# A circular convolution fed tile by tile into an MLP: the inverse transform's chain begins some chunks earlier, and its roundings are queued behind named gelus

## The chip, the core and the metric

The kernel runs on one core of a Trainium2 chip. The metric is device time in microseconds, the median of the runs. Engines are named as the profile names them: PE (TensorE, with its weight loads as PEld), DVE (VectorE), ACT (ScalarE), POOL (GpSimd), SP (SyncE, which here only issues DMAs). Each engine takes its instructions in the order of its own queue. ACT and POOL issue DMAs too, from the same queue as their arithmetic.

## The reference

```python
# 8 batches, 3008 tokens, 256 channels, 2048 hidden
X = np.fft.rfft(x, axis=1)
F = (filt_r + 1j * filt_i)[None, :, :]
y = np.fft.irfft(X * F, n=x.shape[1], axis=1).astype(np.float32)
x = y.reshape(B * S, D)
h = x @ w_in
g = h * (1.0 / (1.0 + np.exp(-1.702 * h)))
out = (g @ w_out).astype(np.float32)
```

All of it is float32. The kernel multiplies float32r parts: a value is rounded to a high part, and the rest is kept as a low part, so that one product becomes three passes (high x high, high x low, low x high).

## The kernel before

The tokens are cut into 48 **tiles** of up to 512 tokens, `tiles[j] = (b, t)`, with batch b = 0 to 7 and t = 0 to 5; a tile with t = 5 and even b is 384 wide. The tiles' MLP is what PE does most of the time. Per tile it runs over NFC = 16 **chunks** of 128 hidden units. For a chunk fc:

- `first(fc)`: six matmuls h<-y,wi (L782) into a PSUM bank of a ring of three (two of its own and one shared); then ACT's gelu twice, gh (L785, rounded) and in place (L786), then DVE's gl = h - gh (L787), after which the bank is free for the next chunk but two.
- `second(fc)`: four matmuls o<-gh,wo and two o<-gl,wo (L806). The two gl matmuls are held back into the next chunk.
- after chunk 15 ACT copies one PSUM bank of o out (L813) and DVE the other (L814), and SP stores them (L824). There are two o banks, so the next tile's `second(0)` needs both copies.

The **turns** loop (L876) numbers all chunks n = 0, 1, 2, ...; from tile 2 on, n = 16 j + fc. In turn n it traces `first` of chunk n + 2 (`ahead`), then `second` of chunk n, then a share of the next batch's forward transform, then steps of the next tile's signal.

**fft(b)** computes the filtered spectrum of batch b while batch b - 1 is in the MLP. For b > 1 its first half is `packed` (s matmuls L537, eviction by ACT L539 and DVE L540/L541, DMA to a_d issued by ACT L468); its second half reads a_d (zy loads issued by POOL L574), has 16 steps of `forward`/`backward` (matmuls L588, merges L596/L597, product L605, L610 to L612, splitting L616/L617) and writes b_d (DMA issued by ACT L633). Its filter comes in f_buf, a pair of buffers that SP loads two steps ahead (`load_f`, issued at L208). It is spread over the turns by a list of costs.

**turned_signal(b, t, y)** (L721), for the 35 tiles with b > 0 and t > 0, makes the tile's input y from b_d. It is a generator; each `yield` ends a step:

1. load: `br` by two DMAs from SP (L731, issued at L208);
2. rounding: for m = 0, 1 ACT copies br to bh (L737), and POOL subtracts bl = br - bh (L738);
3. and 4. passes: for m = 0, 1 three matmuls i<-bh, bl, bh (L305 to L307) and DVE's transpose into zt (L746);
5. write: zt to DRAM (z_d<-zt, SP);
6. reads: four DMAs y<-z_d (SP), into the tile y, which has two buffers;
7. and 8. for m = 0, 1 `split_off` (L714): ACT rounds y's high part (L718), POOL subtracts its low part (L719).

For t = 0, or b = 0, `signal` (L652) does the work with other steps; the change leaves their turns as they are.

Steps of tile i + 1 are run during tile i (the tile ahead of it), in the turns fc of the list `at` (L909): (0, 2, 3, 4, 5, 7, 11, 12) for a turned signal, one step at each.

What sets the order on an engine: the program is traced in the order of the source, and a scheduler then places the instructions into the engines' queues by a simulated timeline, earlier-traced ones first whenever several are ready in it. It may so place an instruction far ahead of where it was traced if its inputs and buffers are ready in the simulation. `keep_in_program_order` pins an instruction against the others that are pinned on its engine (the first matmul of the passes, the transform's matmuls, early loads). br and zt share seven `raw` buffers with the transform, and bh and bl seven `half` buffers.

Of the kernel before, what the change touches and what calls it, by code (L numbers as in the profile page):

```python
# [13 lines left out]
AF = mybir.ActivationFunctionType  # L14
# [153 lines left out]
def tile_kernel(  # L168
# [545 lines left out]
    def split_off(y, m, q, to=None):  # L714

        to = y[:, :, m, q] if to is None else to
        src = y[:, 1, m, q].bitcast(F32)
        nc.scalar.copy(to[:, 0], src)  # L718
        nc.gpsimd.tensor_tensor(to[:, 1], src, to[:, 0].bitcast(F32), ALU.subtract)  # L719

    def turned_signal(b, t, y):  # L721

        if not t2_two:
            t2_two.append(const.tile([P, 2, P], F32R, name="t2_two"))
            nc.scalar.copy(t2_two[0][:, 0], t2_sb)
            nc.vector.tensor_tensor(t2_two[0][:, 1], t2_sb, t2_two[0][:, 0].bitcast(F32), ALU.subtract)
        t2h, t2l = (t2_two[0][:, k] for k in range(2))
        br = raw(f"br_{b}_{t}")
        for j in range(2):
            n = NH * j + 4 * t  # L730
            load_in(br[64 * j : 64 * j + 64], b_of[b][n : n + 4].rearrange("n k d -> k n d"))  # L731
        yield
        es = []
        for m in range(2):
            eh, el = half(f"bh_{b}_{t}_{m}"), half(f"bl_{b}_{t}_{m}")
            src = br[:, 2 * m : 2 * m + 2]
            nc.scalar.copy(eh, src)  # L737
            nc.gpsimd.tensor_tensor(el, src, eh.bitcast(F32), ALU.subtract)  # L738
            es.append((eh, el))
        yield  # L740
        zt = sb.tile([P, 8, 4, 32], F32, tag="raw", name=f"zt_{b}_{t}", bufs=7)
        for m in range(2):
            ps = ring("f", [P, 2, D], f"i1_{b}_{t}_{m}")
            mm3(ps, t2h, t2l, *es[m])
            to = zt[:, :, 2 * m : 2 * m + 2].rearrange("p c q i -> p q c i")
            nc.vector.transpose(to, ps.rearrange("p q (c i) -> p q c i", c=8))  # L746
            yield
        z_d = dram.tile([P, 8, P], F32, tag="z_d", name=f"z_d_{b}_{t}")
        load_in(z_d, zt.rearrange("p c q i -> p c (q i)"))
        yield  # L750
        src = z_d.rearrange("(a j) (k g) e -> g j k a e", a=4, g=4)
        for g in range(4):
            dst = y[32 * g : 32 * g + 32, 1].bitcast(F32)
            load_in(dst.rearrange("p k (a e) -> p k a e", a=4), src[g])
        yield
        for m in range(2):
            if t < 5 or b % 2:
                split_off(y, m, slice(0, 512))
            if t == 5 and b % 2:
                for k in range(2):  # L760
                    gap = slice(352 + 128 * k, 384 + 128 * k)
                    nc.gpsimd.tensor_copy(y[:, :, m, gap], carry[:, :, m, 32 * k : 32 * k + 32].bitcast(F32))
            elif t == 5:
                split_off(y, m, slice(0, 352))
                split_off(y, m, slice(384, 416), y[:, :, m, 352:384])
                split_off(y, m, slice(416, 480), carry[:, :, m])
            yield

    def mlp(b, t, y, nb, sums):

        w = P * nb
        pos, gs, held = [], {}, []

        def first(fc):
            ps = ring("h", [P, 512], f"h_{b}_{t}_{fc}")
            half, o = divmod(fc, HALF)
            c = slice(P * o, P * o + P)  # L780
            for n, (kc, wk, yk) in enumerate([(k, *q) for k in range(2) for q in ((0, 0), (0, 1), (1, 0))]):
                nc.tensor.matmul(ps[:, :w], wi_sb[half][:, wk, kc, c], y[:, yk, kc, :w], start=n == 0, stop=n == 5)  # L782
            gh = sb.tile([P, 512], F32R, tag="gh", name=f"gh_{b}_{t}_{fc}", bufs=3)
            gl = sb.tile([P, 512], F32R, tag="gl", name=f"gl_{b}_{t}_{fc}", bufs=3)
            nc.scalar.activation(gh[:, :w], ps[:, :w], AF.Gelu_apprx_sigmoid)  # L785
            nc.scalar.activation(ps[:, :w], ps[:, :w], AF.Gelu_apprx_sigmoid)  # L786
            nc.vector.tensor_tensor(gl[:, :w], ps[:, :w], gh[:, :w].bitcast(F32), ALU.subtract)  # L787
            gs[fc] = gh, gl

        def second(fc, hold):  # L790
            if fc == 0:
                pos.extend(p.tile([P, 512], F32, tag=k, name=f"o_{b}_{t}_{m}") for m, (p, k) in enumerate(sums))
                if sums[0][0] is ps_x:
                    shared[0] = None
            gp = gs.pop(fc)
            wo = wo_sb[fc // HALF][:, fc % HALF]
            order = held[:]
            order += [(m, wo[:, wk], gp[0], fc == wk == 0, False) for wk in range(2) for m in range(2)]
            if fc == NFC - 1:
                order.sort(key=lambda q: q[0])  # L800
            held[:] = [(m, wo[:, 0], gp[1], False, fc == NFC - 1) for m in range(2)]
            if not hold:
                order += held
                held.clear()
            for m, wb, g, first_one, last_one in order:
                ins = nc.tensor.matmul(  # L806
                    pos[m][:, :w], wb[:, P * m : P * m + P], g[:, :w], start=first_one, stop=last_one
                )
                if (b, t, fc) == (*tiles[-1], NFC - 1):
                    tc.keep_in_program_order(ins)  # L810
            if fc == NFC - 1:
                o = sb.tile([P, 2, 512], F32, tag="out", name=f"out_{b}_{t}")
                nc.scalar.copy(o[:, 0, :w], pos[0][:, :w])  # L813
                nc.vector.tensor_copy(o[:, 1, :w], pos[1][:, :w])  # L814
                for m in (0, 1) if (b, t) == tiles[-1] else (slice(0, 2),):
                    stores.append((out[:, m, done_w[0] : done_w[0] + w], o[:, m, :w]))
                done_w[0] += w

        return first, second
# [6 lines left out]
    def run(gen, n=None):  # L826
        while n is None or n > 0:
            if next(gen, run) is run:
                return False
            n = None if n is None else n - 1  # L830
        return True
# [1 line left out]

    carry = const.tile([P, 2, 2, 64], F32R, tag="carry", name="carry")
    b_t = []
    ys, t2_two = {}, []

    def start(b, t):
        ys[b, t] = sb.tile([P, 2, 2, 512], F32R, tag="y", name=f"y_{b}_{t}")
        return (turned_signal if b and t else signal)(b, t, ys[b, t])  # L840
# [27 lines left out]
    def width(i):  # L868
        return 4 if tiles[i][1] < 5 or tiles[i][0] % 2 else 3

    legs, passed, since = [], 0, 0
    for b in range(B - 1):
        upto = sum(NFC * width(i) for i in range(6 * b + 6)) - 4 * LEAD - (12 * width(6 * b + 5) if b else 26)
# [2 lines left out]
    for n, (i, fc) in enumerate(turns):  # L876
        b, t = tiles[i]
        if n == 0:
            run(start(*tiles[1]))
        if n == 2 * NFC:  # L880
            shared[0] = "f"
        if n == 6 * NFC:
            shared[0] = "h"
        while begun <= min(n + 1 + (n >= 6 * NFC), len(turns) - 1):
            ahead(*turns[begun])
            begun += 1
        chunks_of[i][1](fc, turns[n + 1 : n + 2] == [(i, fc + 1)])
        if fc == 1:
            store()
        if n < 26:  # L890
            run(conv, 1)
            if n % 2 and n < 12:
                load_unit(EARLY + 9 + n // 2)
        if n == 11:
            split_de()
            in_order[0] = False
        if n == 26:
            zy.append(const.tile([P, 4, 2, 2, D], F32R, tag="zy", name="zy"))
        if n >= LEAD and legs:
            passed += width(i)  # L900
            costs, steps, upto = legs[0]
            while steps and sum(costs) - sum(steps) + steps[0] <= sum(costs) * (passed - since) / (upto - since) + 0.01:
                run(nxt[0], 1)
                steps.pop(0)
            if not steps:
                legs.pop(0)
                nxt[0] = fft(B - len(legs)) if legs else None
                since = upto
        at = (0, 2, 3, 4, 5, 7, 11, 12) if t < 5 and b else (1, 3, 9) if t < 5 else (8, 11, 12) if b else (9, 12, 13)  # L909
        if n in (23, 26, 27) or i > 1 and fc in at and i + 1 < len(tiles):  # L910
            i = max(i, 1)
            if i + 1 not in sigs:
                sigs[i + 1] = start(*tiles[i + 1])
            run(sigs[i + 1], 1)
            if n == 27 or i > 1 and fc == at[-1]:
                run(sigs[i + 1])
    store()


# [26 lines left out]
```

## Time and profile before

| | us |
|---|---|
| median of 3 runs (2362.40 to 2367.47) | 2364.46 |
| the profiled execution's own time | 2361.29 |
| its span, first to last instruction | 2359.5 |
| PE busy | 2337.6 (99%) |
| DVE busy | 1612.2 (68%) |
| ACT busy | 1385.0 (59%) |
| POOL busy | 1106.1 (47%) |
| granted TensorE clock | 1.00 |

The profile is one execution. An engine's busy time counts its arithmetic; waits and DMA issues are not in it. PE's matmuls are pipelined, and the end of each is modelled, so that a matmul's shown length is longer than the step from one to the next; an idle time of PE is shown shorter than it is by that difference. A wait is put down to what came last.

### The profile page before, as it was taken

The page shows a single profiled execution, that of the slowest core. Times are in us where ns is not written, and L with a number is a line of the kernel's source. Part 1 is how long each engine was busy: PE and PEld are TensorE (multiplying, and loading weights), DVE is VectorE, ACT ScalarE, POOL GpSimd, SP SyncE. Part 2 cuts the span into 40 slices and gives each one's busy share as a digit, 9 for nine tenths or more (in the row PEclk, how much of TensorE's full clock was granted, in tenths as well). Part 3 has the DMA queues.
Part 4 walks back from the last instruction along what each step waited for, and adds up shares of the span by engine and source line. Part 5 has one row for each costly group of instructions (what it writes and reads, how often), then busy time and mean ns, then how long its engine had stood idle before and what let it go on. Part 6 is the DMA issues. An engine that isn't in the chain of part 4 may idle for free.

```text
span 2359.5 us, 32148 instructions
## 1 busy us (share of the span) xinstructions
PE 2337.6 (99%) x10680; PEld 1945.0 (82%) x10680; DVE 1612.2 (68%) x2476; ACT 1385.0 (59%) x2572; POOL 1106.1 (47%) x979
## 2 busy tenths in 40 slices
PE   9999999999999999999999999999999999999999
PEld 7878898887888878888888877978888888788887
DVE  7978867787676776768767677676876687732322
ACT  6666656566565656656666566565666566544443
POOL 3035546455554555646555455545656455510110
PEclk9999999999999999999999999999999999999999
DMA  9275545565445664465544655455654555421110
GB/s 334 81 196 109 110 108 136 117 150 128 116 134 119 137 134 110 130 136 132 118 131 132 129 118 123 116 149 113 146 135 115 134 130 119 103 59 39 55 41 18
DMA packets 183077, 285.50 MB, mean 121 GB/s; under 512 B 18176, under 2 KB 119680, under 8 KB 182912
## 3 DMA queue, kind: packets, MB, share of 16 engines
q1 hardware_dynamic: 106208, 172.96, 25.5%
q0 software_dynamic: 46592, 44.05, 11.5%
q10 hardware_dynamic: 30112, 66.44, 11.2%
q8 instruction: 85, 1.39, 0.3%
q14 instruction: 80, 0.66, 0.1%
HBM read 171.18 MB, written 112.20 MB: 120 GB/s over the span
## 4 chain that ended last, share of the span: by engine, by line
PE 80%; DVE 4%; DMA 3%; issue 2%; POOL 1%; ACT 1%; SPq 1%; ACTq 0%; DVEq 0%; POOLq 0%
PE o L806 36%; PE h L782 36%; PE i L588 2%; PE s L588 2%; DMA y<-z_d 2%; PE s L537 1%; DVE gl L787 1%; PE i L700 1%; SPq L208 1%; DMA z_d<-zt 1%; DMA br<-b_d 1%; PE i L305 1%; PE i L307 1%; PE i L306 1%; POOL c_buf L612 1%
## 5 line engine op out<-in xcount | busy, mean ns | idle before, releaser
L782 PE MATMUL h<-y,wi 128*128 128x512 f32 (+1 forms) x4608 | 1176.8, 386 | 9.8 <-DVE gl L787 9.3
L782 PEld LDWEIGHTS h<-y,wi 128*128 128x128 f32 x4608 | 857.0, 188 | 180.0 <-DVE gl L787 18.1
L787 DVE TENSOR_TENSOR gl<-h,gh 128x512 fp32r<-128x512 f32 (+1 forms) x768 | 520.1, 679 | 500.9 <-ACT h L786 429.4
L806 PE MATMUL o<-gh,wo 128*128 128x512 f32 (+1 forms) x3072 | 835.8, 385 | 2.7 <-ACT gh L785 2.7
L785 ACT ACTIVATE gh<-h 128x512 fp32r<-128x512 f32 (+1 forms) x768 | 451.9, 588 | 520.8 <-PE h L782 417.8
L806 PEld LDWEIGHTS o<-gh,wo 128*128 128x128 f32 x3072 | 573.7, 188 | 114.1 <-ACT gh L785 4.6
L806 PE MATMUL o<-gl,wo 128*128 128x512 f32 (+1 forms) x1536 | 484.0, 385 | 0.3 <-DVE gl L787 0.3
L786 ACT ACTIVATE h<-h 128x512 f32<-128x512 f32 (+1 forms) x768 | 448.7, 584 | 0.0
L617 POOL TENSOR_TENSOR zy<-c_buf,zy 48x512 fp32r<-48x512 f32 x224 | 319.9, 1428 | 74.5 <-DVE zy L616 64.3
L806 PEld LDWEIGHTS o<-gl,wo 128*128 128x128 f32 x1536 | 287.5, 188 | 56.3 <-DVE gl L787 1.1
L612 POOL TENSOR_TENSOR c_buf<-c_buf,u_buf 112x512 f32<-112x512 f32 x112 | 144.6, 1291 | 260.9 <-DVE c_buf L611 260.9
L738 POOL TENSOR_TENSOR bl<-br,bh 128x512 fp32r<-128x512 f32 x70 | 92.4, 1328 | 289.2 <-ACT bh L737 283.0
L574 POOL DMA_DIRECT2D zy<-a_d x224 | 130.2, 586 | 168.9 <-PE s L588 60.6
L597 DVE TENSOR_TENSOR c_buf<-s,c_buf 48x512 f32<-48x512 f32 x224 | 154.0, 688 | 37.7 <-ACT c_buf L596 32.1
L719 POOL TENSOR_TENSOR y<-y 128x512 fp32r<-128x512 f32 (+1 forms) x76 | 90.7, 1212 | 169.4 <-ACT y L718 169.4
L597 DVE TENSOR_TENSOR b<-i,b 48x512 f32<-48x512 f32 x224 | 153.6, 686 | 19.2 <-ACT b L596 13.9
L596 ACT COPY c_buf<-s 48x512 f32<-48x512 f32 x224 | 130.2, 581 | 55.9 <-PE s L588 27.0
L596 ACT COPY b<-i 48x512 f32<-48x512 f32 x224 | 130.1, 581 | 40.5 <-PE i L588 32.1
L539 ACT CAST a<-s 64x512 fp32r<-64x512 f32 x144 | 83.7, 581 | 83.9 <-PE s L537 51.4
L616 DVE CAST zy<-c_buf 48x512 fp32r<-48x512 f32 x224 | 97.1, 434 | 49.9 <-POOL c_buf L612 45.5
L540 DVE TENSOR_TENSOR a<-s,a 64x512 f32<-64x512 f32 x144 | 99.0, 688 | 46.4 <-ACT a L539 43.4
L526 POOL TENSOR_TENSOR e<-x,e 64x512 fp32r<-64x512 f32 x72 | 94.7, 1316 | 46.6 <-DVE e L525 25.0
(128 smaller groups left out, 1779.1 us busy)
## 6 DMA issues: line engine op xcount, KB each, us to landing
f_buf<-fs SPq DMA_DIRECT2D x224, 192.0 KB, 3.4
zy<-a_d POOLq DMA_DIRECT2D x224, 192.0 KB, 3.6
a_d<-a ACTq DMA_DIRECT2D x144, 256.0 KB, 3.0
x<-in_x_dram SPq DMA_DIRECT2D x47, 512.0 KB, 5.3
out_dram<-out SPq DMA_DIRECT2D x43, 512.0 KB, 3.6
b_d<-b ACTq DMA_DIRECT2D x112, 192.0 KB, 2.6
br<-b_d SPq DMA_DIRECT2D x84, 256.0 KB, 4.5
z_d<-zt SPq DMA_DIRECT2D x35, 512.0 KB, 2.7
```

The source lines that it names most:

```text
L540: nc.vector.tensor_tensor(lo, ps[t], a[t, 0], ALU.subtract)
L574: nc.gpsimd.dma_start(zy[0][64 * k : 64 * k + 48, i % 2].rearrange("p k s d -> p (k s) d"), src)
L596: nc.scalar.copy(dst[h], ps[o])
L597: nc.vector.tensor_tensor(dst[h], ps[h], dst[h], ALU.add)
L612: nc.gpsimd.tensor_tensor(u1, u1, u2, ALU.add)
L616: nc.vector.tensor_copy(y[h, k], u1[h])
L617: nc.gpsimd.tensor_tensor(y[o, k], u1[h], y[h, k].bitcast(F32), ALU.subtract)
L782: nc.tensor.matmul(ps[:, :w], wi_sb[half][:, wk, kc, c], y[:, yk, kc, :w], start=n == 0, stop=n == 5)
L785: nc.scalar.activation(gh[:, :w], ps[:, :w], AF.Gelu_apprx_sigmoid)
L786: nc.scalar.activation(ps[:, :w], ps[:, :w], AF.Gelu_apprx_sigmoid)
L787: nc.vector.tensor_tensor(gl[:, :w], ps[:, :w], gh[:, :w].bitcast(F32), ALU.subtract)
L806: ins = nc.tensor.matmul(pos[m][:, :w], wb[:, P * m : P * m + P], g[:, :w], start=first_one, stop=last_one)
```

## The change

A list `gelu` collects every second gelu instruction (L786) as it is traced. Two kinds of ACT copies of the turned signal, the rounding (L737) and the one of `split_off` (L718), are traced inside `tc.issue_after(gelu[-1])`: on ACT's queue they stand behind the newest gelu traced so far, wherever else the scheduler puts them. No semaphore is added, since both are on ACT. In turn n the newest traced gelu is that of chunk n + 2.

The turns of the steps are no longer read from the tile that runs, but listed ahead in `due`, by the tile j that they are for, counted from the first turn of the tile ahead, 16 (j - 1). For a turned signal they become (-6, -2, -1, 0, 1, 3, 9, 10) instead of (0, 2, 3, 4, 5, 7, 11, 12): the load 6 turns earlier, rounding, passes, write and reads 4 earlier, `split_off` 2 earlier. The first steps so lie in the last turns of the tile before the tile ahead. The other signals keep their turns.

```diff
@@ split_off
-        nc.scalar.copy(to[:, 0], src)
+        with tc.issue_after(gelu[-1]):
+            nc.scalar.copy(to[:, 0], src)
@@ turned_signal
-            nc.scalar.copy(eh, src)
+            with tc.issue_after(gelu[-1]):
+                nc.scalar.copy(eh, src)
@@ mlp, first
-            nc.scalar.activation(ps[:, :w], ps[:, :w], AF.Gelu_apprx_sigmoid)
+            gelu.append(nc.scalar.activation(ps[:, :w], ps[:, :w], AF.Gelu_apprx_sigmoid).ins)
@@ tile_kernel
-    ys, t2_two = {}, []
+    ys, t2_two, gelu = {}, [], []
...
+    due = {}
+    for j in range(2, len(tiles)):
+        b, t = tiles[j]
+        if j == 2:
+            steps = 23, 26, 27
+        else:
+            at = (-6, -2, -1, 0, 1, 3, 9, 10) if b and t else (1, 3, 9) if t else (8, 11, 12) if b > 1 else (9, 12, 13)
+            steps = [NFC * (j - 1) + k for k in at]
+        for n in steps:
+            due.setdefault(n, []).append(j)
...
-        at = (0, 2, 3, 4, 5, 7, 11, 12) if t < 5 and b else (1, 3, 9) if t < 5 else (8, 11, 12) if b else (9, 12, 13)
-        if n in (23, 26, 27) or i > 1 and fc in at and i + 1 < len(tiles):
-            i = max(i, 1)
-            if i + 1 not in sigs:
-                sigs[i + 1] = start(*tiles[i + 1])
-            run(sigs[i + 1], 1)
-            if n == 27 or i > 1 and fc == at[-1]:
-                run(sigs[i + 1])
+        for j in due.pop(n, ()):
+            if j not in sigs:
+                sigs[j] = start(*tiles[j])
+            run(sigs[j], 1)
+            if not any(j in later for later in due.values()):
+                run(sigs[j])
```

## Rows read from the trace of the kernel before

**Rows 1.** The page, busy time of each engine (share of the span) and instructions.
```profile
PE 2337.6 (99%) x10680; PEld 1945.0 (82%) x10680; DVE 1612.2 (68%) x2476; ACT 1385.0 (59%) x2572; POOL 1106.1 (47%) x979
```

**Rows 2.** Busy time by stretch: from:to, length, busy (instructions) per engine, clock, DMA.
```profile
340.00:2060.00 1720.00, 1705.77 (x7661) 1417.84 (x7660) 1245.02 (x1894) 1039.65 (x1915) 940.01 (x831) 1.00 0.53 127
...
2160.00:2220.00 60.00, 60.00 (x267) 1.00 0.12 36
```

**Rows 3.** Waits of PE, 340 to 2060 us: total us, times, longest us.
```profile
PE h L782 <- DVE gl L787: 8.9, 9, 2.6
PE i L588 <- POOL zy L617: 2.9, 9, 0.5
```

**Rows 4.** Groups of PE's instructions by form: busy us, mean ns, idle before.
```profile
L782 PE MATMUL h<-y,wi 128*128 128x512 f32 x4224 | 1096.7, 390 | 6.7 <-DVE gl L787 6.6
```

**Rows 5.** Waits, whole span, the two of ACT that a DMA ended.
```profile
ACT y L718 <- DMA y<-z_d: 79.5, 34, 5.1
...
ACT bh L737 <- DMA br<-b_d: 50.8, 17, 5.6
```

**Rows 6.** SP's timeline: start, us, line, DMA, how many [idle before].
```profile
539.45 8.19 SPq L208 DMA_DIRECT2D f_buf<-fs  x4
547.68 1.28 SPq L208 DMA_DIRECT2D br<-b_d  x2
...
871.60 0.34 SPq L208 DMA_DIRECT2D z_d<-zt  x1
874.29 2.58 SPq L208 DMA_DIRECT2D y<-z_d  x4
```

**Rows 7.** ACT's timeline, in five places.
```profile
553.67 0.62 ACT L737 CAST bh<-br 128x512 fp32r<-128x512 f32 x1 [5.58 <-DMA br<-b_d]
...
793.26 0.62 ACT L737 CAST bh<-br 128x512 fp32r<-128x512 f32 x1 [2.24 <-DMA br<-b_d]
...
796.74 0.59 ACT L813 COPY out<-o 128x512 f32<-128x512 f32 x1
...
882.12 0.61 ACT L718 CAST y<-y 128x352 fp32r<-128x352 f32 x2 [4.64 <-DMA y<-z_d]
...
987.39 0.59 ACT L813 COPY out<-o 128x512 f32<-128x512 f32 x1 [1.04 <-DVE a L541]
```

**Rows 8.** PE's timeline, in the same places.
```profile
556.18 1.67 PE L782 MATMUL h<-y,wi 128*128 128x512 f32 x6 [2.64 <-DVE gl L787]
...
794.71 4.24 PE L782 MATMUL h<-y,wi 128*128 128x512 f32 x18
...
888.93 0.50 PE L588 MATMUL i<-zy,de_sb 128*128 128x512 f32 x1 [0.46 <-POOL zy L617]
...
988.95 0.61 PE L806 MATMUL o<-gh,wo 128*128 128x512 f32 x2
```

**Rows 9.** Busy time by stretch behind ten long waits of ACT, PE first.
```profile
553.60:566.10 12.50, 9.92 (x44) 8.19 (x44) 9.16 (x15) 9.97 (x18) 8.87 (x9) 1.00 0.69 139
843.40:855.90 12.50, 11.62 (x49) 8.79 (x49) 8.85 (x14) 11.08 (x21) 7.25 (x7) 1.00 0.56 138
882.10:900.00 17.90, 16.56 (x75) 13.29 (x74) 13.93 (x22) 12.39 (x28) 11.24 (x12) 1.00 0.20 51
...
1374.10:1386.60 12.50, 10.64 (x48) 8.43 (x46) 9.76 (x16) 9.98 (x18) 8.26 (x7) 1.00 0.50 126
...
sum 141.30, PE 129.57 PEld 102.02 DVE 104.43 ACT 104.07 POOL 97.39; mean PE 12.96 PEld 10.20 DVE 10.44 ACT 10.41 POOL 9.74
```

**Rows 10.** The rounding's instructions: duration ns min/median/max, first and last start.
```profile
L737 ACT CAST bh<-br x70: 603/620/627, 361.6 to 2238.9; 128x512 fp32r<-128x512 f32 x70
...
L738 POOL TENSOR_TENSOR bl<-br,bh x70: 1260/1292/1819, 362.4 to 2240.4; 128x512 fp32r<-128x512 f32 x70
```

**Rows 11.** Timelines of POOL and of DVE behind the wait at 882 us.
```profile
887.36 3.19 POOL L617 TENSOR_TENSOR zy<-c_buf,zy 48x512 fp32r<-48x512 f32 x2 [0.53 <-DVE zy L616]
...
887.76 1.66 DVE L605 TENSOR_TENSOR u_buf<-c_buf,f_buf 48x512 f32<-48x512 f32 x1
```

## The prediction

> **What bounds the kernel now.** First the page's busy times: PE is at 99%, the next engine at 68% [rows 1]. So no other engine can be the bound as a whole, and this change removes no matmul. What it can give back is time in which PE stands still. The second view is therefore PE's busy time by stretch: between 340 and 2060 us, where the turned signals run beside the transforms, PE is idle for 1720 - 1705.77 = 14.2 us; behind it, with no transform left, 60 us hold 60 us of work [rows 2]. Third, PE's waits there: it waits for DVE's gl (a bank of h that is not yet free) or for POOL's zy, 18 times [rows 3], and never for bh, bl or y themselves. The idle time is shown too short: a matmul is drawn 0.390 us long [rows 4], but one follows the other every 60/267 = 0.225 us [rows 2], so each idle time hides 0.165 us more.
>
> Fourth, why is gl late? ACT's waits name the turned signal twice: 79.5 us in 34 waits for the reads of y, and 50.8 us in 17 for the load of br [rows 5]. Most of them cost nothing, as ACT is 59% busy. But ACT works in order: while it stands at a copy whose DMA is out, the gelus behind it stand too, then gl, then the bank, then PE. The timelines show both kinds. At 553.67 ACT has stood 5.58 us at the rounding [rows 7], and PE then stands 2.64 us [rows 8]. At 882.12 it has stood 4.64 us at `split_off` [rows 7]; there PE's loss comes 7 us later, at zy [rows 8], since POOL's splitting is behind as well. A wait of 2.24 us at 793 [rows 7] leaves PE running, with three chunks of h in a row [rows 8]. So the point from which a wait of ACT reaches PE lies between about 2 and 5 us.
>
> Fifth, why are the DMAs late? SP's own queue. The load of br at 547.68 goes out the moment that the f_buf loads ahead of it have ended their 8.19 us, most of it waiting for a free half of f_buf [rows 6]; the rounding's place on ACT was chosen without that. The reads follow the write after 2.7 us (871.60 to 874.29, [rows 6]), and `split_off` stands at ACT some 8 us after the reads began, waiting.
>
> **The change part by part.** Instructions, bytes and matmuls stay the same. Only places change.
>
> Load and rounding: load 6 turns earlier, rounding 4 earlier, hence two turns more between them; and the rounding can no longer slip ahead of the gelu of chunk 0 of the tile ahead. A turn is twelve matmuls, 12 x 0.225 = 2.7 us, and some 3 us with the transform's matmuls in it. Even the 8.19 us that SP stood at f_buf [rows 6] then end before the rounding's place. I take the 50.8 us of [rows 5] as gone, up to a few short waits.
>
> Write, reads and `split_off`: the first two move by 4 turns, the last by 2, and it is held behind the gelus of chunks 11 and 12. The distance grows by two turns, about 6 us, more than the longest wait of 5.1 us in [rows 5]. I take the 79.5 us as gone too. y is then ready about chunk 13, before PE's first matmul of its tile. The tile y has two buffers, and the reads (turn 3 of the tile ahead) come after the last use of the one that they overwrite; SP stands at no new wait for it. SP's write now stands near the store of the finished tile instead of in mid-tile; the store has nobody waiting for it, and the f_buf loads behind the write were behind a write before, too.
>
> What that is worth on PE: ten stretches of 12.5 to 18 us, each begun at the end of an ACT wait of 3.6 us or more, hold 141.30 - 129.57 = 11.7 us of idle PE [rows 9], nearly all of the 14.2. With 18 idle times in them, as many as [rows 3] counts, the hidden part is 18 x 0.165 = 3.0, so 14.7 us in all. Three of the ten are like the one at 882 (17.90 - 16.56 = 1.34 idle each, some 5.5 with the hidden part): there the loss is at zy, and the transform might be late there for reasons of its own. I credit half of these, 2.7 less: **12.0 us gained**, between 6 and 14.7.
>
> What the new places cost. The rounding's two copies, 0.62 us each [rows 10], now stand right behind the first gelu of the tile ahead, before ACT's copy of the last o. For a price there are rows on both sides. At 793 us they already stand there, after a wait of 2.24 us, the out copy follows at 796.74 [rows 7], and PE goes on without a pause [rows 8]: cost 0. In the packed half of the transform, at 987, ACT's copy ends at 987.98 [rows 7], and the next o starts at 988.95 [rows 8]: 0.97 of slack against 1.24, so 0.27 per boundary at most if nothing else moves. There are two such boundaries in each of six transforms: 0 to 3.2 us. A gain is possible as well where the copies leave a fuller place. I take 1.0, nearer to the row with 0, as ACT has waited in all these places before.
>
> The passes now follow the rounding at the same distance on PE, but the rounding cannot run ahead any more, so PE might wait for bl. No row shows such a wait; the nearest is PE waiting for POOL's other subtract, 2.9 us in 9 waits of at most 0.5 [rows 3], over 420 matmuls. For 70 passes that is 70/420 x 2.9 = 0.5 us; ends 0 and 35 x 0.5 = 17 if every tile waits once. I take 0.5, since the scheduler places the passes by the same simulation that it used for zy.
>
> **Sum.** 2361.3 - 12.0 + 1.0 + 0.5 = 2350.8 for the profiled execution, of which the span is 2359.5. That execution is 3.2 us under the median of the runs, 2364.46; on that basis 2364.5 - 10.5 = **2354.0 us**.
>
> One row speaks of POOL against DVE. DVE's product at 887.76 took 1.66 us [rows 11], beside a POOL subtract that began at 887.36 [rows 11]. The Trainium skill (SBUF — State Buffer, "Who interferes with whom") says that a DVE instruction with two inputs in SBUF contends with a GpSimd instruction that reads SBUF, and that the one that comes second waits out the other; this row agrees. By that rule the moved subtracts of POOL would hold up DVE at the tile's boundary; without it, nothing is added. What that would make is the fourth rival below.
>
> **The rivals.** (a) *The load does not really move*: where a raw buffer or SP's f_buf wait, not the traced turn, decides when br goes out, it goes out no sooner, and the rounding goes on waiting. For it: br went out right behind f_buf [rows 6]. Against it: six turns are two f_buf periods. Then only the waits for y go: the three stretches with a br wait hold 2.58 + 0.88 + 1.86 = 5.3 us [rows 9], 6 with the hidden part, so 12.0 - 6.0 - 1.5 = 4.5 is left: 2360.0. (b) *Nothing in the end*: ACT's waits go, but the shifted order of transform and MLP makes as many losses of PE elsewhere, in the manner of the 2.9 us at zy [rows 3]: 2364. (c) *The boundary becomes the bound*, the case on the other side. The two copies go before the out copy and the next gelu in all 35 tiles; PE has two o banks, and three banks of h as cover. About ten tiles have the rounding there today (the one at 793, [rows 7], is typical). In the other 25 the loss could lie between 0.27 (with the slack of 987) and 1.24 (with none); in the middle 0.75 x 25 = 19, hence 2364.5 - 12 + 19 = 2371.5. It decides from (12.0 + 4.7)/25 = 0.67 us per boundary. Against it stands the row at 794.71. (d) *POOL's subtracts hold DVE*: two product steps per boundary, each longer by 1.66 less a usual 0.69, are 1.9 us on DVE; if half of that reaches PE at the 18 boundaries in the transforms' second half (35 less the 12 in the first half and the 5 of the last batch, which has no transform beside it), 17 us: 2369.5. Against it: gl and the out copy read only one operand from SBUF.
>
> **How the numbers follow.** A measurement of this kernel can tell about 0.2%, 4.7 us, so faster is below 2359.7, and slower above 2369.2. Forecast 0.64; (a) 0.13, which lies on the edge, a third of it faster; (b) 0.10; (c) 0.09; (d) 0.04. Faster 0.64 + 0.04 = 0.68; slower 0.13; same 0.19. The range: below, the full 14.7 and the 2.5 us of other idle time, 2364.5 - 17.2, so 2347; above, it takes in (a) and (b) and the near part of (c) and (d): 2367. Some 8 in 10 lie in it; the forecast's own range is 2348 to 2359.
>
> **What would show it.** The waits of ACT for br and y fall from 130 us to under 20. PE's idle time between 340 and 2060 us falls from 14.2 us to 3 to 5, and the 2.64 at 556 has no equal. SP issues br during the last six chunks before the tile ahead begins. ACT's rounding follows the first gelu of the tile ahead. For (c) PE's waits for gl or for the out copy would come once per tile, in the first 5 us of it, 25 times or more; for (d) L605, L610 and L611 would have a longer mean; for (a) the waits for br would stay near 50 us. The forecast is wrong if PE's idle time does not fall although ACT's waits do: then the threshold of 2 to 5 us was read wrongly, or the transform's order makes the losses.

## The result, and the profile after

The changed kernel takes **2340.16 us** (median of 4 runs, 2339.54 to 2340.87) against 2364.57 for the kernel before on the same chip (2362.40 to 2367.47): a ratio of 0.9894, 95% interval 0.9880 to 0.9909. That is 24.4 us less; the forecast was 10.5 less, and the range ended at 2347. The profiled execution took 2339.9 us, its span 2338.1.

The page's busy times, and PE's busy time by stretch, which answer to [rows 1, 2]:

```profile
PE 2327.7 (100%) x10680; PEld 1947.3 (83%) x10680; DVE 1672.0 (72%) x2476; ACT 1388.7 (59%) x2572; POOL 1111.4 (48%) x979
...
340.00:2060.00 1720.00, 1717.51 (x7789) 1441.82 (x7789) 1314.86 (x1912) 1054.07 (x1941) 952.01 (x836) 1.00 0.52 128
```

PE's idle time between 340 and 2060 us fell from 14.2 us to 2.5. The view of PE's waits in that stretch has a single row left (total us, times, longest), and a wait for zy is not in it. Before, the same view had 21 waits: the 18 of [rows 3], and two more rows that neither [rows 3] nor the prediction has. First the two rows of before, then the one of after:

```profile
PE o L806 <- ACT gh L785: 1.5, 2, 1.1
PE s L588 <- DVE b L597: 0.4, 1, 0.4
...
PE h L784 <- DVE gl L789: 2.5, 2, 1.3
```

ACT's waits hold no row for br or for y any more, where [rows 5] show 50.8 and 79.5 us. How a chain now runs is seen in SP's and ACT's timelines around the boundary at 546 us, the same boundary as the 553.67 of [rows 7]. Line numbers are those of the changed kernel: matmuls h L784 and o L808, gelus L787 and L788, gl L789, rounding L739, out copies L815 and L816, `split_off` L719 and L720.

```profile
517.81 8.92 SPq L208 DMA_DIRECT2D f_buf<-fs  x3
526.77 1.27 SPq L208 DMA_DIRECT2D br<-b_d  x2
...
546.19 0.59 ACT L788 ACTIVATE h<-h 128x512 f32<-128x512 f32 x1
546.70 0.60 ACT L739 CAST bh<-br 128x512 fp32r<-128x512 f32 x1
547.33 0.58 ACT L596 COPY b<-i 48x512 f32<-48x512 f32 x1
547.94 0.62 ACT L739 CAST bh<-br 128x512 fp32r<-128x512 f32 x1
...
550.30 0.59 ACT L815 COPY out<-o 128x512 f32<-128x512 f32 x1
```

br still goes out right behind an f_buf load that held SP for 8.92 us, as in [rows 6], but 20 us before the rounding instead of 6. The rounding stands behind the gelu of the tile's first chunk and waits for nothing; PE runs through without a pause.

Where the time came from is seen in ACT's out copies, one per tile, at the end of each batch (start in us, read from ACT's timelines of both kernels):

| out copy of the ..th tile | 6 | 12 | 18 | 24 | 30 | 36 | 42 | 48 |
|---|---|---|---|---|---|---|---|---|
| before | 355.6 | 648.6 | 936.0 | 1226.9 | 1514.6 | 1805.6 | 2090.7 | 2355.3 |
| after | 356.4 | 645.7 | 928.1 | 1217.0 | 1499.3 | 1788.3 | 2069.9 | 2333.9 |
| gained so far | -0.8 | 2.9 | 7.9 | 9.9 | 15.3 | 17.3 | 20.9 | 21.4 |

Nothing is gained before the first turned signal, 2 to 5 us in each batch with one, and almost nothing in the last batch, which has no transform beside it.

### The profile page after: what moved, and what is told of

It reads as the page before. It is cut to its first block, busy times and chain, and to the rows that moved or that the text cites. A ratio compares the mean times of both kernels' runs of the same rounds, so it can differ in the third digit from the quotient of the medians.

```text
span 2338.1 us, 32186 instructions
## 1 busy us (share of the span) xinstructions
PE 2327.7 (100%) x10680; PEld 1947.3 (83%) x10680; DVE 1672.0 (72%) x2476; ACT 1388.7 (59%) x2572; POOL 1111.4 (48%) x979
## 4 chain that ended last, share of the span: by engine, by line
PE 91%; DMA 0%; DVE 0%; issue 0%; POOL 0%; ACT 0%; SPq 0%; ACTq 0%; POOLq 0%; DVEq 0%
PE h L784 41%; PE o L808 41%; PE s L588 2%; PE i L588 2%; PE s L537 1%; PE i L700 1%; PE i L305 1%; PE i L307 1%; PE i L306 1%; DMA x<-in_x_dram 0%; POOL ev L519 0%; DVE gl L789 0%; ACT gh L787 0%; PE bt L671 0%; PE s L585 0%
## 5 line engine op out<-in xcount | busy, mean ns | idle before, releaser
L784 PE MATMUL h<-y,wi 128*128 128x512 f32 (+1 forms) x4608 | 1181.9, 385 | 3.0 <-DVE gl L789 2.9
L784 PEld LDWEIGHTS h<-y,wi 128*128 128x128 f32 x4608 | 857.5, 188 | 168.1 <-DVE gl L789 5.0
L808 PE MATMUL o<-gh,wo 128*128 128x512 f32 (+1 forms) x3072 | 835.3, 385 | 1.3 <-ACT gh L787 1.2
L787 ACT ACTIVATE gh<-h 128x512 fp32r<-128x512 f32 (+1 forms) x768 | 452.8, 590 | 620.4 <-PE h L784 480.9
L789 DVE TENSOR_TENSOR gl<-h,gh 128x512 fp32r<-128x512 f32 (+1 forms) x768 | 520.1, 679 | 419.8 <-ACT h L788 399.4
L808 PEld LDWEIGHTS o<-gh,wo 128*128 128x128 f32 x3072 | 573.5, 188 | 112.1 <-ACT gh L787 2.3
L808 PE MATMUL o<-gl,wo 128*128 128x512 f32 (+1 forms) x1536 | 479.5, 385 | 0.5 <-DVE gl L789 0.5
L788 ACT ACTIVATE h<-h 128x512 f32<-128x512 f32 (+1 forms) x768 | 448.6, 584 | 0.0
L808 PEld LDWEIGHTS o<-gl,wo 128*128 128x128 f32 x1536 | 287.4, 188 | 56.5 <-DVE gl L789 1.4
L720 POOL TENSOR_TENSOR y<-y 128x512 fp32r<-128x512 f32 (+1 forms) x76 | 95.2, 1259 | 190.5 <-ACT y L719 170.0
L597 DVE TENSOR_TENSOR b<-i,b 48x512 f32<-48x512 f32 x224 | 153.8, 687 | 11.6 <-ACT b L596 6.3
L616 DVE CAST zy<-c_buf 48x512 fp32r<-48x512 f32 x224 | 117.7, 525 | 39.3 <-POOL c_buf L612 34.8
L605 DVE TENSOR_TENSOR u_buf<-c_buf,f_buf 48x512 f32<-48x512 f32 x112 | 108.4, 968 | 3.7
```

The lines of the kernel that those rows point to most:

```text
L597: nc.vector.tensor_tensor(dst[h], ps[h], dst[h], ALU.add)
L605: nc.vector.tensor_tensor(u2[64:Q], u1[0:48], f_i[0:48], ALU.mult)
L616: nc.vector.tensor_copy(y[h, k], u1[h])
L788: gelu.append(nc.scalar.activation(ps[:, :w], ps[:, :w], AF.Gelu_apprx_sigmoid).ins)
L808: ins = nc.tensor.matmul(pos[m][:, :w], wb[:, P * m : P * m + P], g[:, :w], start=first_one, stop=last_one)
```

## The experiments

"PE's loss" below is worked out from the starts of PE's matmuls: where one starts more than 0.377 us after the one before it (a 512-wide step takes 0.227), what is over 0.227 counts, from 340 us on. It is told behind which wait of ACT for br or y it stands: the longest one that ended up to 13 us ahead. That a loss stands behind a wait is an order in time and not yet a cause. Waits are total / longest in us, from the view of ACT's waits.

Each ratio is against the kernel before on the same chip. e1, e5 and e6 ran on one chip (before: median 2362.4, from 2358.0 to 2371.0 in 13 runs), e2, e3, e4 and e8 on a second (2364.9), e7, e9, e10 and e11 on a third (2364.8). Medians of different chips, and a ratio and a difference of medians, can so differ by 2 to 5 us.

| kernel | median us | ratio, 95% interval | waits for br | for y | PE's loss behind waits of 3 us or more | its other loss |
|---|---|---|---|---|---|---|
| before | 2364.6 | | 50.8 / 5.6 | 79.5 / 5.1 | 14.6 | 4.3 |
| the change | 2340.2 | 0.9894, 0.9880 to 0.9909 | none | none | 0 | 2.8 |
| e1_turns_only | 2349.5 | 0.9928, 0.9909 to 0.9947 | 44.7 / 6.5 | 58.5 / 4.4 | 2.7 | 5.6 |
| e2_issue_only | 2350.8 | 0.9935, 0.9921 to 0.9950 | 5.5 / 2.6 | 7.2 / 2.7 | 0 | 11.6 |
| e5_load_only | 2369.4 | 1.0021, 1.0006 to 1.0035 | 26.9 / 4.5 | 79.4 / 6.3 | 12.4 | 14.6 |
| e6_chain_only | 2344.6 | 0.9905, 0.9886 to 0.9925 | 27.0 / 5.5 | 62.5 / 5.3 | 4.4 | 1.3 |
| e3_load_late | 2346.5 | 0.9919, 0.9902 to 0.9935 | 20.9 / 3.0 | none | 1.3 | 7.5 |
| e8_load_mid | 2351.6 | 0.9941, 0.9926 to 0.9955 | 14.2 / 3.6 | none | 0.4 | 14.1 |
| e4_split_early | 2350.9 | 0.9937, 0.9922 to 0.9952 | none | 74.4 / 5.5 | 9.8 | 1.7 |
| e9_queue_rounding | 2348.6 | 0.9928, 0.9913 to 0.9943 | none | 69.2 / 5.3 | 7.3 | 1.6 |
| e10_queue_split | 2341.9 | 0.9902, 0.9885 to 0.9919 | 34.3 / 3.9 | none | 0 | 4.4 |
| e7_twice | 2338.8 | 0.9889, 0.9874 to 0.9904 | none | none | 0 | 2.1 |
| e11_queue_packed | 2340.1 | 0.9892, 0.9877 to 0.9907 | none | none | 0 | 1.8 |

### The kernel before, a second profile

> The kernel before once more, unchanged, for a second profile. If the waits for DMAs vary from one execution to the next and PE's loss with them, a profiled execution that takes 2364 to 2367 us shows 2 to 5 us more PE idle and hidden time than the one of 2361.3 us, behind the same kind of waits; if the difference of 3.2 us between that execution and the median lay elsewhere (start and end), PE's idle time is the same 22 us.

Its time was 2363.8 us, its span 2362.0, 2.5 over the profile of [rows 2]. The waits of ACT are the same to about 1 us (49.7 for br, 80.3 for y), and the stalls of PE stand at nearly the same places: the one of [rows 8] at 556 lost 3.13 us here and 2.81 there. PE's loss is 20.3 us, 1.4 more than in the first profile; most of the rest of the 2.5 had come about before 504 us. So the kernel before varies from run to run in part by the size of its stalls.

### The two halves of the change

e1_turns_only has the new turns and no queueing; e2_issue_only the old turns and both queueings.

```diff
 e1_turns_only, at both places
-            with tc.issue_after(gelu[-1]):
-                nc.scalar.copy(eh, src)
+            nc.scalar.copy(eh, src)
 e2_issue_only
-            at = (-6, -2, -1, 0, 1, 3, 9, 10) if b and t else ...
+            at = (0, 2, 3, 4, 5, 7, 11, 12) if b and t else ...
```

> The changed turns without the queueing: rounding and split_off may again be placed anywhere on ACT. Theory A (the distances between load and rounding and between reads and split_off are what ended ACT's waits): the waits of ACT for br and y stay under 40 us of the 130 us of before, and the time is 2340 to 2347 us. Theory B (the queueing behind the gelu is what did it, since the scheduler otherwise moves the copies up to where its simulation has the DMA landed): the waits come back to 60 us or more and the time is over 2350 us. Theory C (neither; the reordering of transform and MLP by chance): no relation between ACT's waits and the time.

> The queueing without the new turns: the steps at (0, 2, 3, 4, 5, 7, 11, 12), each rounding and split_off behind its named gelu, here that of chunk 4 for the rounding and of chunks 13 and 14 for split_off. Theory A (ACT's waits for br and y, by their total): they fall from 130 us to under 40, and the time follows them unless y now comes too late: 2345 to 2352 us. Theory D (new, after the load alone gained nothing and the chain alone 18 us with ACT still waiting 98 us: it counts where on ACT a wait stands, at the tile's boundary or in mid-tile): the waits that are left stand in mid-tile, PE gains about as well, 2345 to 2355. Against both: y is split off behind chunk 14, some 3 us before PE's first matmul of the tile needs it, and PE may wait for POOL's y once per tile, 35 x 1 us or more: over 2360.

Each alone gives some 60% of the gain (15.0 and 13.8 us of 24.4 by the table's medians; by the ratios 17.0 and 15.4 of 25.1). With the turns alone the scheduler places the rounding 2 to 7 chunks ahead of the boundary in 28 of the 35 tiles, and 103 us of waits are left: theory A is out, and B's 60 us are there, with a time just under its 2350. The longest waits for br now stand in mid-tile: the longest of all, 6.51 us at 537, cost PE 0.19. With the queueing alone the waits fall as theory A had it (12.7 us left, none over 2.8), and the time lies in its range, yet PE loses 11.6 us. That is the first mark against the thought that the sum of ACT's waits is the price: e6 below has 90 us of them and is 6 us faster. Of the 11.6 us, 6.7 stand in one place, between 599.6 and 614.9, where `split_off` and POOL's subtracts, at the end of the old turns, reach the boundary. A wait of ACT for y stands ahead of it, of only 2.75 us, and the largest stall comes 14.5 us behind it, outside the 13 us of the table; so this loss may still hang on a wait. ACT, PE, DVE and POOL there:

```profile
596.59 1.14 ACT L719 CAST y<-y 128x512 fp32r<-128x512 f32 x2 [2.75 <-DMA y<-z_d]
...
608.16 0.50 PE L588 MATMUL i<-zy,de_sb 128*128 128x512 f32 x1 [0.73 <-POOL zy L617]
611.10 2.71 PE L784 MATMUL h<-y,wi 128*128 128x512 f32 x6 [2.44 <-DVE gl L789]
...
607.01 1.65 DVE L610 SCALAR_TENSOR_TENSOR u_buf<-c_buf,f_buf 48x512 f32<-48x512 f32 x1
608.69 1.64 DVE L611 TENSOR_TENSOR c_buf<-c_buf,f_buf 112x512 f32<-112x512 f32 x1
610.36 1.89 DVE L789 TENSOR_TENSOR gl<-h,gh 128x512 fp32r<-128x512 f32 x3
...
606.60 3.18 POOL L617 TENSOR_TENSOR zy<-c_buf,zy 48x512 fp32r<-48x512 f32 x2 [2.61 <-DVE zy L616]
```

Two DVE steps of 1.65 us, usually 0.7, while POOL's two subtracts run; gl queues behind them, three at once, and PE behind gl.

### The load alone, and the rest of the chain alone

No queueing; of the new turns only the load's, or all others with the load 4 earlier like them.

```diff
 e5_load_only
+            at = (-6, 2, 3, 4, 5, 7, 11, 12) if b and t else ...
 e6_chain_only
+            at = (-4, -2, -1, 0, 1, 3, 9, 10) if b and t else ...
```

> The kernel before, with the load alone 6 turns earlier (turns -6, 2, 3, 4, 5, 7, 11, 12), no queueing. Theory A: the waits for br fall from 50.8 us to under 15, those for y stay near 80 us; PE gets back what lay behind the br waits, three stretches of 5.3 us of idle time and about 3 us hidden: 2354 to 2358 us. Theory C: 2340 (any reordering) or 2364 (none of it).

> Load, rounding, passes, write and reads all 4 turns earlier, split_off 2 (turns -4, -2, -1, 0, 1, 3, 9, 10), no queueing; load and rounding so keep the distance that they had before. Theory A: the waits for y go (under 15 us of 79.5), those for br stay at 30 us or more; PE gets back what lay behind the y waits, 6.4 us of idle time in seven stretches and about 6 hidden: 2348 to 2354 us. Theory C: 2340 or 2364.

The load alone halves the waits for br (under 15 us were expected) and makes the kernel 5 us slower, where theory A had it faster: the waits for y stay, and the reordered transform has new stalls behind no long wait of ACT (1.99 us at 503, 1.22 at 804, 1.23 at 1385). The moved chain alone gives 20.0 of the 24.4 us (17.8 against the median of before on its own chip, 22.5 by the ratio), with 90 us of waits left. It went against its expectation: the waits for y did not go (62.5 us), and the time is better than the range. One of the waits is as long as the 5.58 us of [rows 7], but in mid-tile. ACT's and PE's timelines:

```profile
1062.68 0.62 ACT L737 CAST bh<-br 128x512 fp32r<-128x512 f32 x1 [5.47 <-DMA br<-b_d]
...
1063.40 1.52 PE L782 MATMUL h<-y,wi 128*128 128x512 f32 x6
1064.76 0.62 PE L806 MATMUL o<-gl,wo 128*128 128x512 f32 x2
1065.22 1.09 PE L806 MATMUL o<-gh,wo 128*128 128x512 f32 x4
1066.14 0.39 PE L588 MATMUL i<-zy,de_sb 128*128 128x512 f32 x1
1067.05 0.50 PE L588 MATMUL s<-zy,de_sb 128*128 128x512 f32 x1 [0.52 <-DVE c_buf L597]
```

PE has work on hand for all of the 5.47 us and loses 0.68 behind it. At the boundary, where the out copies stand in the same queues, 5.58 us cost 2.81. The pair alone does not show that the place decides (see below).

### The load's place, with the queueing

e3_load_late puts the load at -2, together with the rounding; e8_load_mid puts load to second pass at -7, -7, -6, -5, -4.

```diff
 e3_load_late
+            at = (-2, -2, -1, 0, 1, 3, 9, 10) if b and t else ...
 e8_load_mid
+            at = (-7, -7, -6, -5, -4, 3, 9, 10) if b and t else ...
```

> The changed kernel with the load put into the rounding's own turn (-2 instead of -6): the rounding still stands behind the gelu of chunk 0, at the tile's boundary, and has to wait for the load there. Theory A and D: ACT waits for br in nearly every tile, 2 us or more at a time where SP stands at f_buf, 60 us in all; PE loses at the boundary: 2347 to 2360 us. Theory C (order by chance): within 3 us of 2340.

> The changed kernel with load and rounding in one turn as in the run with the load late, but the two, the passes and the write five turns earlier (turns -7, -7, -6, -5, -4, 3, 9, 10): the rounding waits for its load behind the gelu of chunk 11 of the tile before, in mid-tile. Theory D: ACT waits as much as with the load late at the boundary, and PE loses less than half of what it loses there: 2340 to 2347 us. Theory A: the same loss for the same wait.

In e3_load_late the waits for br came back as 20.9 us and not as 60, none over 3.0, and two of them cost some 2 us, where a pass on PE waited for bh itself. More came from elsewhere: the two stalls that the change has left (below) grew from 1.4 to 2.6 and 2.8 us. So both theories' 60 us and 2347 were missed. e8_load_mid missed its expectation: with 14.2 us of waits it is 11 us slower than the change. Its losses (2.75 at 934, 2.93 at 1510, 1.27 at three places) stand behind no wait of ACT for br or y. A different order of the same work has stalls of its own.

### `split_off` earlier

```diff
+            at = (-6, -2, -1, 0, 1, 3, 4, 5) if b and t else ...
```

> The changed kernel with split_off at turns 4 and 5 instead of 9 and 10, behind the gelus of chunks 6 and 7, where the reads have hardly landed (they do at chunk 6.0 to 8.9). Theory A: ACT waits for y 2 us or more in most tiles, 80 us or more in all, and PE loses as it did before: 2350 to 2360 us. Theory D: the same waits in mid-tile cost a third of that: 2342 to 2348 us.

Only the distance between reads and `split_off` is undone, five turns of it. The waits for y are back, 32 of them, 74.4 us, and with them PE's losses: 9.8 of its 11.5 us stand behind five of the six waits of over 4 us; the waits of 3 to 3.71 us cost PE nothing. That is theory A's time and not theory D's, though the waits stand in mid-tile. The largest of the losses, 5.0 us at 583 to 587, holds some 1.4 us that came from a lower clock (last section).

### One queueing at a time

```diff
 e9_queue_rounding, in split_off
-        with tc.issue_after(gelu[-1]):
-            nc.scalar.copy(to[:, 0], src)
+        nc.scalar.copy(to[:, 0], src)
 e10_queue_split, in turned_signal
-            with tc.issue_after(gelu[-1]):
-                nc.scalar.copy(eh, src)
+            nc.scalar.copy(eh, src)
```

> The changed kernel, but only the rounding is queued behind a named gelu; the copy of split_off is free again. With neither queued and the same turns (the run of the turns alone) the time was 2349.5, 9.2 above the change: br was waited for 44.7 us (longest 6.5) and y 58.5 us (longest 4.4). If long waits of ACT cost and short ones do not, nearly all of the 9.2 belongs to the rounding: here br is under 5 us in all, y is waited for 50 to 80 us but never much over 4.4, and the time is 2340 to 2344. If each queueing is worth its waits by their sum, the waits for y cost 58.5/103 of the 9.2: 2345 to 2346. If it is the order as a whole that decides, the time has no relation to either and shows stalls of PE that stand behind no wait of ACT.

> The changed kernel, but only the copy of split_off is queued behind a named gelu; the rounding is free again. Counterpart of the run before. By the long waits: the rounding is placed ahead of its turn as in the run of the turns alone, br is waited for 30 to 50 us with several waits over 4 us, y for under 5 us, and the time is 2346 to 2350. By the sum of the waits: 2340.2 + 9.2 x 45/103 = 2344. By the order as a whole: anything from 2342 to 2352, with stalls not behind waits of ACT.

Both went against the first of the readings expected: the queueing of `split_off` is worth 7.6 of the 9.3 us between the turns alone and the change, that of the rounding 1.0 (by the ratios 6.1 and 0.0 of 8.0). By the length of the waits it fits: without the rounding's queueing 34.3 us of waits for br remain, but the longest is 3.91, and PE loses nothing behind any of 3 us or more. Without that of `split_off`, four waits for y of 4.0 to 5.28 us appear, and losses of PE behind three of them, at zy again behind the longest two (1057 and 1630 us). The first of them, with 5.0 of the 8.8 us that PE loses here, shows how the loss comes about; ACT, POOL, DVE and PE in turn, and then the stretch behind it (from:to, length, busy of PE with count, the other engines, clock):

```profile
573.53 1.14 ACT L718 CAST y<-y 128x512 fp32r<-128x512 f32 x2 [4.00 <-DMA y<-z_d]
...
574.28 1.29 POOL L719 TENSOR_TENSOR y<-y 128x512 fp32r<-128x512 f32 x1 [6.96 <-ACT y L718]
...
580.08 2.95 POOL L617 TENSOR_TENSOR zy<-c_buf,zy 48x512 fp32r<-48x512 f32 x2
...
580.28 1.63 DVE L605 TENSOR_TENSOR u_buf<-c_buf,f_buf 48x512 f32<-48x512 f32 x1
581.93 1.64 DVE L610 SCALAR_TENSOR_TENSOR u_buf<-c_buf,f_buf 48x512 f32<-48x512 f32 x1
583.61 0.69 DVE L788 TENSOR_TENSOR gl<-h,gh 128x512 fp32r<-128x512 f32 x1
...
584.35 2.93 PE L783 MATMUL h<-y,wi 128*128 128x512 f32 x6 [3.31 <-DVE gl L788]
...
584.35:587.50 3.15, 3.15 (x7) 2.48 (x8) 2.59 (x5) 0.18 (x1) 1.99 (x2) 0.50 0.51 125
```

ACT is late by 4.0 us; POOL's queue, which stood at the same signal for 6.96, then runs without a pause; two DVE steps fall on its subtracts and take 1.63 each; gl stands behind them, and PE stands 3.31 us, until 10.8 us after ACT went on. I read this from the traces; no run took POOL's part away alone.

### Twice the rounding

```diff
             with tc.issue_after(gelu[-1]):
                 nc.scalar.copy(eh, src)
+                nc.scalar.copy(eh, src)
```

> The changed kernel, with each rounding copy bh<-br written twice, behind the same gelu: 70 more ACT copies of 0.62 us, 1.24 us more of ACT at the start of each of the 35 tiles ahead, before the out copy. Rival (c) of the prediction prices this place at 0.27 to 1.24 us of PE per boundary; by its middle (0.75 x 25 to 35) the second pair would cost 19 to 26 us: 2359 to 2366, with PE waiting for an o bank or for gl in the first 5 us of most tiles. If ACT has cover there, as in the changed kernel's trace, where no such wait stands, the time is 2340 to 2344 and PE's shown idle time between 340 and 2060 us stays under 5 us. Between the two: the cover is between 1.24 and 2.5 us.

2338.8 us (2338.33 to 2340.03): no loss, and no gain that could be told from the change's own runs. ACT's timeline at the boundary that was shown above, with the copy twice:

```profile
545.49 0.61 ACT L739 CAST bh<-br 128x512 fp32r<-128x512 f32 x1
546.12 0.59 ACT L596 COPY b<-i 48x512 f32<-48x512 f32 x1
546.60 0.62 ACT L740 CAST bh<-br 128x512 fp32r<-128x512 f32 x1
547.25 0.58 ACT L596 COPY b<-i 48x512 f32<-48x512 f32 x1
547.85 0.63 ACT L739 CAST bh<-br 128x512 fp32r<-128x512 f32 x1
...
550.12 0.60 ACT L740 CAST bh<-br 128x512 fp32r<-128x512 f32 x1
550.62 0.59 ACT L816 COPY out<-o 128x512 f32<-128x512 f32 x1
```

PE's only waits between 340 and 2060 us are two for gl, 1.9 us together, at 898 and 1469 us, neither of them once per tile. Four copies, 2.5 us of ACT, find cover at the boundary: rival (c) is refuted, for twice its cost.

### The two stalls that are left

What remains of PE's loss stands at 1182 and 1753 us. DVE, POOL and PE at the first:

```profile
1178.44 2.75 DVE L525 CAST e<-ev 64x512 fp32r<-64x512 f32 x1 [2.53 <-POOL ev L519]
1181.22 1.29 DVE L789 TENSOR_TENSOR gl<-h,gh 128x512 fp32r<-128x512 f32 x2
...
1177.12 1.29 POOL L519 TENSOR_TENSOR ev<-x 128x512 f32<-128x512 f32 x1 [7.52 <-DMA x<-in_x_dram]
1178.36 1.30 POOL L612 TENSOR_TENSOR c_buf<-c_buf,u_buf 112x512 f32<-112x512 f32 x1
1179.61 1.29 POOL L519 TENSOR_TENSOR x<-x 128x512 f32<-128x512 f32 x1
...
1181.96 1.65 PE L784 MATMUL h<-y,wi 128*128 128x512 f32 x6 [1.23 <-DVE gl L789]
```

The same pattern without ACT: a cast of the packed transform, placed ahead of two gl, waits for POOL and a late load, and is then held by two POOL instructions besides (2.75 us, where the shortest of its line takes 0.42). e11_queue_packed uses the change's own means on it.

```diff
-            nc.vector.tensor_tensor(gl[:, :w], ps[:, :w], gh[:, :w].bitcast(F32), ALU.subtract)
+            gls.append(nc.vector.tensor_tensor(gl[:, :w], ps[:, :w], gh[:, :w].bitcast(F32), ALU.subtract).ins)
...
-                    (nc.vector.tensor_copy if h else nc.scalar.copy)(es[n, h][t], src[t])
+                    with tc.issue_after(gls[-1] if h else gelu[-1]):
+                        (nc.vector.tensor_copy if h else nc.scalar.copy)(es[n, h][t], src[t])
```

> The changed kernel, and the same means used on the two stalls of PE that it has left past 340 us (1180.7 and 1752.0, each 1.2 us shown): there DVE stood 2.5 us at a cast of the packed transform (e<-ev) that waits for POOL and a late load, and the cast itself took 2.75 us, with two gl behind it. Here the casts e of `split` are queued on DVE behind the newest gl traced, and on ACT behind the newest gelu. If a queue that stands at a hoisted instruction is the cause, both stalls go and the time falls by 2 to 4 us: 2336 to 2339. If the places matter only as one order among many, new stalls of 1 to 3 us appear elsewhere in the packed half and the time is 2340 to 2350. The casts of the transform then go later to PE, and PE might wait for e (s<-e): that would be shown as such.

Both stalls are gone, as meant: at 1178.45 and 1179.46 gl now runs by itself. The time is 2340.05 us, no different: smaller stalls (0.64 at 930 and 1501) and steps lengthened by less than 0.15 us took their place. No version was found that is faster than the change by more than can be measured.

## Why the prediction was too small

**The step that failed** is the size of PE's loss in the sum. The prediction put what the change gives back at 12.0 us, and at no more than 17.2 in the range, by the drawn idle time plus 0.165 us at each of 18 waits. By the starts of the matmuls PE lost 24.1 us from 340 us on (18.9 in 28 long steps, 5.2 in shorter ones), and 3.8 in the changed kernel (2.8 and 1.0).

**What was right.** The place of the idle time (PE behind gl and zy, [rows 3, 9]; the two rows shown above, with 1.9 us, were left out), its cause (ACT standing at DMAs of the turned signal, [rows 5, 7]) and the sign. The marks named ahead came: ACT's waits are under 20 us (none), PE's idle time is 2.5 us (a little under the 3 to 5 forecast), br goes out well before the tile ahead, the rounding follows the first gelu. Rival (a) is out, since br's waits went although SP still stands at f_buf; (b) is out for the whole change, but e2, e5 and e8 show that it was no idle thought: each has fewer waits than before, and 11 to 15 us of loss that stands behind no wait of 3 us or more (in e2, 6.7 of it follows one of 2.75); (c) is out by e7_twice.

**The point of 2 to 5 us** can be given more closely. Over the kernel before, the change and the eleven variants of it, past 340 us: of 205 waits of ACT for br or y under 3 us, 10 have a loss of PE behind them (8.4 us in all, some of it by other causes); of 38 between 3 and 4 us, 9 (9.1 us, about half of it the stall at 584 of e9_queue_rounding, behind a wait of 4.00); of 36 of 4 us and more, 31 (43.7 us). So from some 4 us on a loss is the rule. The sum of the waits decides little (e6 against e2); the length of the single wait does more. That a boundary makes a wait dearer is not shown: of the 36, the five that end behind the gelu of chunk 15 or 0 have 1.3 us of loss behind them in the mean, the other 31 have 1.2. Nor does the loss follow the length: 6.51 us in e1 cost 0.19, and 4.00 in e9 cost 5.0.

**Where the sizes failed.** The span fell by 21.4 us, where the sum had 10.5. The terms of the sum, each with what it measured:

- *The stall's own size.* The ten stretches of [rows 9] were put at 14.7 us (idle time, and 0.165 hidden at 18 waits). From the starts of the matmuls they hold 18.4: 15.2 in 20 long steps, and 3.2 in steps lengthened by less than 0.15 us, which no view shows as idle time. The waits of PE in them are 14, and not 18. Most of the shorter lengthenings stand right behind a stall: the first matmul is drawn 0.50 us long instead of 0.390. That row was at hand (888.93 in [rows 8], beside [rows 4]) and was not read for it. **3.7 us.**
- *Half credit for the zy stretches.* All three went, and the change has no wait for zy left. That they hung on the waits for y is shown by e9_queue_rounding and e4_split_early, where waits for y over 4 us bring losses at zy back. **2.7 us.**
- *The costs*, 1.0 for the boundary and 0.5 for bl: nothing of either in the trace of after, and e7_twice has room for twice the rounding. The slack of 0.97 at 987 ([rows 7, 8]) was no bound, since the out copy there stood behind a wait of its own. **1.5 us.**
- *Stalls outside the ten stretches.* They were credited in the range's end only. Past 340 us before had 3.7 us there in 8 long steps and 2.6 in shorter ones, after has its two stalls of 2.8 and 1.0 in shorter ones: 2.5 us. The sum of these terms needs **3 us** here; the last half of a microsecond is not accounted for.
- *The offset between profile and median.* 3.2 us were carried over as a constant. They went with the change: its four runs lie within 1.4 us, their median 0.3 from its profile, while the kernel before varies over 5 us beside them. That they belong to the stalls is shown only in part: of the 2.5 us that the second profile of before is longer, 1.4 are loss of PE past 340 us. **3 us**, and so 24.4 instead of 21.4.

**Rival (d)** half came true, with other instructions than its own. DVE's busy time rose by 60 us [rows 1]. Of this L616 has 20.6, e's casts at L525 23.6, and the products that I priced only 15.4: L605 8.4 (mean 0.893 to 0.968), L610 4.4, L611 2.6. The groups of L525 on DVE, before and then after (count, shortest/median/longest ns):

```profile
L525 DVE CAST e<-ev x36: 418/425/902, 328.9 to 1845.2; 64x512 fp32r<-64x512 f32 x36
L525 DVE CAST e<-x x36: 415/425/1516, 332.2 to 1849.7; 64x512 fp32r<-64x512 f32 x36
...
L525 DVE CAST e<-ev x36: 424/612/2749, 329.7 to 1840.9; 64x512 fp32r<-64x512 f32 x36
L525 DVE CAST e<-x x36: 418/812/1499, 357.2 to 1842.7; 64x512 fp32r<-64x512 f32 x36
```

gl kept its mean of 0.679 us, as the row against (d) had it. The Trainium skill (SBUF — State Buffer, "Who interferes with whom") also says that a copy or cast on DVE in a two-port mode contends with GpSimd, and that the one that comes second waits for the whole instruction; I had used only its sentence on two inputs. The casts at L525 and L616, one input each, agree with it here. The price on PE was not once per boundary but two stalls of 1.4 us.

What stays open: whether POOL's backlog, DVE's held steps or ACT's wait itself is the larger part of a loss such as the one in e9_queue_rounding; the traces show all three in a chain. For br there is no run that brings its long waits back alone, as e4_split_early and e9_queue_rounding do for y: that they cost PE is read from the stretches of before and of e1. And why a given order has its own single stalls (e2, e8) can be told only afterwards, from its trace.

## What to carry to other kernels

An in-order engine that stands at an instruction whose DMA is still out costs little while the engine that it feeds still has work on hand, here mostly up to 4 us; so look for the longest single waits, not at their sum, and check in the trace what each of them cost. Move the whole chain earlier and pin its copies behind named instructions of the main loop together: each alone gave some 60% of the gain, and moving the load alone made a loss. And size a stall by the starts of the instructions, not by the idle time drawn: the drawn 14.2 us of PE's idle time were 24.1 by the starts.

## What the hardware showed besides

A stall of PE can be paid a second time through its clock. Behind the 3.31 us of e9_queue_rounding the granted clock is 0.50 in the stretch shown above, the 1.2 GHz level, and six matmuls take 2.93 us instead of 1.52, so 1.4 us on top. The same is behind the 3.51 us of e4_split_early, 2.59 and 2.77 in e8_load_mid, 2.65 in e3_load_late and 2.44 in e2_issue_only (611.10, shown above). Behind 2.64 us in the kernel before (556.18, [rows 8]) the six take 1.67 and the clock stays at 1.00, and so it does behind the same stall in the second profile, though that one is 2.97 us long. There PE and then the stretch behind it, and last the stretch behind the 2.44 us of e2_issue_only:

```profile
557.34 1.67 PE L782 MATMUL h<-y,wi 128*128 128x512 f32 x6 [2.97 <-DVE gl L787]
557.40:560.70 3.30, 3.30 (x15) 2.68 (x16) 2.90 (x5) 2.42 (x5) 2.15 (x3) 1.00 0.47 147
...
611.40:614.70 3.30, 3.30 (x9) 2.53 (x8) 2.19 (x5) 0.85 (x2) 1.73 (x2) 0.50 0.91 273
```

So the drawn length of the stall alone does not tell whether the clock falls, and these runs do not show what does.
